# One core, attention and MLP: the first pair's decay inside its q k product, and a new order of the early loads

## The chip, the core and the metric

The kernel runs on one core of a Trainium2 chip. The core has a TensorE (PE, matrix products, with its weight loads PEld), a VectorE (DVE), a ScalarE (ACT), a GpSimd (POOL) and a SyncE (SP). POOL and SP issue the DMA transfers of this kernel; transfers from POOL may change the type from float32 to float16 on the way, those from SP may not. The metric is the device time in microseconds (us) of one execution, the median of several.

## The reference

For each of 8 batches and 8 heads (sequence S = 576, head size D = 64):

```python
scores = scale * np.matmul(q, k.transpose(0, 1, 3, 2))
log_f = np.log(np.clip(f, 0.0001, 1.0))
cum = np.cumsum(log_f, axis=-1)
decay = cum[:, :, :, None] - cum[:, :, None, :]
scores = np.where(causal, -1000000000.0, scores + decay)
attn = softmax(scores)            # exp(scores - max) / (sum + 1e-09)
x = (attn @ v), heads side by side: 4608 rows of 512
h = x @ w_in                      # 512 -> 2048
out = (h - np.tanh(h)) @ w_out    # 2048 -> 512
```

So a score of query s and key t needs q.k, plus a number that depends on s alone (cum at s), minus one that depends on t alone (cum at t).

## The kernel before, in words

**Pairs and tiles.** The work of attention is cut into 32 pairs: batch b, heads 2c and 2c+1. The scores of a pair lie with keys on partitions, in seven tiles `ti` of up to 512 columns (`TILES`, L289: tiles 0 to 2 are head 0, tile 3 holds the last 64 keys of both heads, tiles 4 to 6 are head 1). `scores` (L306) writes one tile into one of two PSUM buffers with PE and lets ACT take the exponential (L335). In batch 0 the causal mask is added by PE (a product of the identity with `late`, L329); later batches are masked by POOL. `trans` (L254) transposes q or k of the next pair on PE and has the result copied to `QT` and `KT` (L275 on ACT, L277 on DVE). `values` (L350) multiplies by v and `turn` (L369) transposes the result for the MLP.

**Decay.** f of all 64 batch-heads is loaded at once (L123), clipped (L150), put through Ln (L157) and summed along the sequence (a scan, L159). From `cum` come three rows for every head: `chi` (cum times 8, in float16), `clo` (what float16 lost of it) and `cq` (for the query side). For every pair but the first, these rows are copied by DMA into rows 64 to 66 of `KT` and `QT` (`load_aug`, L168), beside rows of 1 and -1 (`const_rows`, L175), and one product over 67 rows gives q.k and decay together. The first pair can't wait for that transfer: there `decay_part` (L294) adds the decay in two more products per piece of a tile (L295 with `dec`, which holds chi and clo for all heads, and a two-column selector `sel`; L297 with `cq` and a column of the identity), and the product of q and k (L326) has 64 rows.

**Order.** From `start` (L521) on, all five engines execute exactly in the order in which the program issues (`manual_schedule`, L604, L606); the lines above it (loads, constants, Ln, scan) are ordered by the scheduler. `unread(n)` (L512) issues n products of a constant tile that nobody reads, where PE would otherwise stand idle. `att_items` (L547) lists the work of pair p: while the scores of pair p are made, the transposes of pair p+1 (at tiles `at_q`, `at_k`) and the values of pair p-1 go in between, and `LOADS` (L196) says at which tile which load is issued by POOL. From pair 4 on, products of the MLP are dealt among the items (`TAKE`, L601).

**Loads.** POOL issues loads one after the other. There are eight completion semaphores for its transfers, used in turn, so that the ninth transfer waits until the first has landed. In the prologue POOL issues q and k of heads 0-1 and 2-3, the v parts of the first heads, then (`bulk`, L181) q of heads 4-7, the three rows of decay, k of heads 4-7 and four blocks of v. Then come, by `LOADS`, q and k of batch 1, the first half of `w_in` (`win`, 1024 KB), v of batch 1, the second half of `w_in`, `w_out`.

Of the kernel before, what the change touches and what calls it, by code (L numbers as in the profile page):

```python
# [14 lines left out]
PITCH = 640  # L15
# [6 lines left out]
def kernel(  # L22
# [95 lines left out]
    def load_v_block(b, n, h0, h1):  # L118
# [3 lines left out]
    lf = TQ[0][0:NH, :, :].rearrange("p c s -> p (c s)").bitcast(FP32)[:, 0:S]  # L122
    nc.sync.dma_start(out=lf, in_=f.rearrange("b h s -> (b h) s"))  # L123
    load_qk(qn, q, 0, 0, 2)
    load_qk(kn, k, 0, 0, 2)
# [4 lines left out]
    nc.gpsimd.affine_select(out=id16, in_=id16, compare_op=ALU.not_equal,  # L130
                            fill=1.0, base=0, pattern=[[-1, P]], channel_multiplier=1)
    load_qk(qn, q, 0, 2, 4)
    load_qk(kn, k, 0, 2, 4)
    ones16 = TK[0:NH, 0, :]
    sel = cst.tile([P, 2], FP16)
    dec = cst.tile([P, PITCH], FP16)
# [5 lines left out]
    nc.vector.memset(dec[:, S:PITCH], 0.0)  # L142
# [6 lines left out]

    nc.vector.tensor_scalar(out=lf, in0=lf, scalar1=0.0001, scalar2=1.0,  # L150
                            op0=ALU.max, op1=ALU.min)

    nc.vector.scalar_tensor_tensor(out=sel, in0=id16[:, 0:2], scalar=-1.0, in1=id16[:, NH:NH + 2],
                                   op0=ALU.mult, op1=ALU.subtract)
    nc.vector.memset(vn[0][D:P, NJ - 1, :, :], 0.0)
    nc.vector.memset(vn[0][:, :, :, D:VW], 1.0)
    nc.scalar.activation(out=lf, in_=lf, func=AF.Ln)  # L157
    cum = TQ[0][0:NH, :, :].rearrange("p c s -> p (c s)").bitcast(FP32)[:, S:2 * S]
    nc.vector.tensor_tensor_scan(out=cum, data0=ones16, data1=lf, initial=0.0,  # L159
                                 op0=ALU.mult, op1=ALU.add)  # L160
    chi = dec[0:NH, 0:S]
    nc.vector.tensor_scalar_mul(out=chi, in0=cum, scalar1=inv_qscale)
    cq = cst.tile([NH, S], FP16)
    expo = cst.tile([1, 1], FP32)
    clo = dec[NH:2 * NH, 0:S]
    nc.vector.scalar_tensor_tensor(out=clo, in0=cum, scalar=inv_qscale, in1=chi,
                                   op0=ALU.mult, op1=ALU.subtract)
    def load_aug(b):  # L168
        i, hs = b % 2, slice(b * H, (b + 1) * H)
        eng = nc.gpsimd if b == 0 else nc.sync  # L170
        eng.dma_start(out=KT[i][D:D + 1, :, 0:S], in_=chi[hs, :])
        eng.dma_start(out=QT[i][D + 2:D + 3, :, :], in_=cq[hs, :])
        eng.dma_start(out=KT[i][D + 1:D + 2, :, 0:S], in_=clo[hs, :])
# [7 lines left out]
    def bulk():  # L181
        load_qk(qn, q, 0, 4, H)
# [111 lines left out]
    def decay_part(ps, a, j, i0, n, col):  # L294
        nc.tensor.matmul(out=ps[:, col:col + n], lhsT=dec[:, j * P:(j + 1) * P],  # L295
                         rhs=sel[:, a:a + 1].to_broadcast([P, n]), start=True, stop=False)
        nc.tensor.matmul(out=ps[:, col:col + n], lhsT=id16[0:NH, a:a + 1].to_broadcast([NH, P]),  # L297
                         rhs=cq[:, i0:i0 + n], start=False, stop=False)

    FIRST = []  # L300

    def decay(ti):
        FIRST.append(ps_sc.tile([P, 512], FP32, tag="sc", name="ps"))
        decay_part(FIRST[0], *TILES[ti][0])

    def scores(b, c, ti):  # L306
        if FIRST:
            ps = FIRST.pop()
        elif b == 0 and ti == LAST:
# [9 lines left out]
        own = b == 0 and c == 0  # L319
        rows = D if own else D + 3  # L320
        for a, j, i0, n, col in TILES[ti]:
            h = 2 * c + a
            if own and ti > 0:
                decay_part(ps, a, j, i0, n, col)
            cut = min(P, n) if b == 0 and i0 == j * P else 0
            nc.tensor.matmul(out=ps[:, col:col + n], lhsT=KT[b % 2][0:rows, h, j * P:(j + 1) * P],  # L326
                             rhs=QT[b % 2][0:rows, h, i0:i0 + n], start=not own, stop=cut == 0)
            if cut:
                nc.tensor.matmul(out=ps[:, col:col + cut], lhsT=id16, rhs=late[:, 0:cut],  # L329
                                 start=False, stop=True)  # L330
# [4 lines left out]
        nc.scalar.activation(out=e[:, lo:hi], in_=ps[:, lo:hi], func=AF.Exp, scale=qscale)  # L335
# [185 lines left out]
    def start():  # L521
        unread(33)
        q_rest = trans(*pairs[0], qn, QT, True, "AAAA", True)
        nc.scalar.activation(out=cq, in_=cum, func=AF.Copy, bias=-SHIFT * inv_qscale, scale=inv_qscale)
        nc.scalar.activation(out=expo, in_=lf[0:1, 0:1], func=AF.Exp)
        unread(6)
        k_rest = trans(*pairs[0], kn, KT, True, "VVVV", True)
# [7 lines left out]
        scores(*pairs[0], 1)  # L535
        q_rest[1]()
        for e in EL[0:2]:
            nc.vector.memset(e, 0.0)
        nc.vector.memset(KT[0][:, :, S:PITCH], 0.0)
# [7 lines left out]
    def att_items(p):  # L547
# [8 lines left out]
        for ti in range(len(TILES)):  # L556
# [5 lines left out]
            if early and p > 0 and ti in (0, 6):  # L562
                put(unread, 2)
# [4 lines left out]
            at_q, at_k = (1, 3) if p == 0 else (0, 1) if early else (0, 2) if p == NPAIR else (0, 3)  # L568
# [34 lines left out]
    FIVE = {PE, mybir.EngineType.Pool, mybir.EngineType.SP, mybir.EngineType.DVE, mybir.EngineType.Activation}  # L603
    with tc.manual_schedule(engines=FIVE):  # L604
        start()
    with tc.manual_schedule(engines=FIVE):  # L606
        bulk()
        for p in range(len(pairs) + 1):
            b, c = divmod(p, NPAIR)
            items = att_items(p)  # L610
            take = TAKE[p] if p < len(TAKE) else 8 - (p - len(TAKE)) % 2
            if p == 2 * NPAIR + 1:
                widen(1)
            mine = mlp[at:at + take]
            at += take
            first = 14 if p == NPAIR else 0
            if p == len(pairs):
                for fn, *args in mine[0:2]:
                    fn(*args)
                mine = mine[2:]  # L620
            given, n = 0, 0
            whole = sum(counts for _, counts in items)
            for emit, counts in items:
                emit()
                n += counts
                while n > first and given < len(mine) and given * (whole - first) < (n - first) * len(mine):
                    fn, *args = mine[given]
                    fn(*args)
                    given += 1
        widen(2)  # L630
        for fn, *args in mlp[at:]:
            fn(*args)
# [28 lines left out]
```

## Time and profile before

| what | value |
|---|---|
| median of 3 runs | 347.94 us (347.92 to 347.96) |
| the profiled execution, its own time | 347.95 us |
| its span in the profile | 346.2 us |
| PE busy | 335.2 us (97%) |
| DVE busy | 261.7 us (76%) |
| ACT busy | 232.6 us (67%) |
| POOL busy | 161.3 us (47%) |
| DMA, all queues | 38.80 MB, mean 112 GB/s |
| granted TensorE clock | 1.0 in every slice |

Between the span and the execution's own time lie 1.75 us. PE is busy nearly throughout, but a busy PE is not a PE at its peak: its products overlap and their ends are modelled. The first 5 us of the span hold the loads and the way from f to `cum`; the first pair lies at about 8 to 16 us, pairs 1 to 3 at 16 to 30 us, and from 32 us on the MLP is dealt in.

### The profile page before, as it was taken

The page shows a single profiled execution, that of the slowest core. Times are in us where ns is not written, and L with a number is a line of the kernel's source. Part 1 is how long each engine was busy: PE and PEld are TensorE (multiplying, and loading weights), DVE is VectorE, ACT ScalarE, POOL GpSimd, SP SyncE. Part 2 cuts the span into 40 slices and gives each one's busy share as a digit, 9 for nine tenths or more (in the row PEclk, how much of TensorE's full clock was granted, in tenths as well). Part 3 has the DMA queues.
Part 4 walks back from the last instruction along what each step waited for, and adds up shares of the span by engine and source line. Part 5 has one row for each costly group of instructions (what it writes and reads, how often), then busy time and mean ns, then how long its engine had stood idle before and what let it go on. Part 6 is the DMA issues. An engine that isn't in the chain of part 4 may idle for free.

```text
span 346.2 us, 8606 instructions
## 1 busy us (share of the span) xinstructions
PE 335.2 (97%) x3253; PEld 230.6 (67%) x3253; DVE 261.7 (76%) x504; ACT 232.6 (67%) x437; POOL 161.3 (47%) x319
## 2 busy tenths in 40 slices
PE   8988998889999999999999999999999999999995
PEld 7476554555578656865688888755875587487485
DVE  6599787564988788678867886788677766876874
ACT  5687886777897787778767876788548842632640
POOL 8974652676558655765577465742322210000000
PEclk9999999999999999999999999999999999999999
DMA  8999999999999999799979997991131013003003
GB/s 108 147 182 201 193 201 154 107 114 177 132 130 105 177 137 122 94 176 137 117 78 200 130 128 78 186 143 27 49 97 31 17 50 110 0 14 109 0 11 113
DMA packets 144877, 38.80 MB, mean 112 GB/s; under 512 B 128148, under 2 KB 143236, under 8 KB 144836
## 3 DMA queue, kind: packets, MB, share of 16 engines
q0 software_dynamic: 92480, 18.39, 69.7%
q1 hardware_dynamic: 52356, 19.88, 30.5%
q8 instruction: 25, 0.41, 0.5%
q14 instruction: 16, 0.13, 0.1%
HBM read 36.85 MB, written 9.44 MB: 134 GB/s over the span
## 4 chain that ended last, share of the span: by engine, by line
PE 87%; DVE 6%; ACT 4%; issue 1%; DMA 1%; ACTq 0%
PE hps L408 32%; PE ops L466 28%; PE ps L326 12%; PE av L357 8%; PE ops L442 3%; DVE gq L417 2%; ACT e L335 2%; DVE QT L277 2%; PE t L264 1%; DVE KT L277 1%; PE ps L329 1%; DMA TQ<-in_f_dram 1%; PE ps L297 1%; ACT QT L275 1%; ACT th L413 1%
## 5 line engine op out<-in xcount | busy, mean ns | idle before, releaser
L408 PE MATMUL hps<-XR,win 128*128 128x512 f16 (+1 forms) x640 | 140.9, 357 | 0.9 <-ACT XR L378 0.7
L413 ACT ACTIVATE th<-hps 128x512 f32<-128x512 f32 x144 | 86.9, 603 | 55.4 <-PE hps L408 54.6
L335 ACT ACTIVATE e<-ps 128x512 f16<-128x512 f32 x192 | 110.5, 598 | 14.1 <-PE ps L326 6.0
L417 DVE TENSOR_TENSOR gq<-hps,th 128x512 f16<-128x512 f32 x144 | 98.4, 688 | 26.0 <-ACT th L413 24.6
L345 POOL TENSOR_SCALAR_AFFINE_SELECT e<-e 128x128 f16<-128x128 f16 x168 | 60.4, 361 | 78.0 <-ACT e L335 76.1
L408 PEld LDWEIGHTS <-win 128*128 128x128 f16 x640 | 57.7, 97 | 48.4 <-issue 0.5
L326 PE MATMUL ps<-QT,KT 67*128 67x64 f16 (+5 forms) x384 | 77.9, 276 | 3.1 <-ACT e L335 1.7
L466 PEld LDWEIGHTS <-gq 128*128 128x128 f16 x640 | 60.4, 97 | 11.1
L466 PE MATMUL ops<-wout,gq 128*128 128x256 f16 x512 | 63.2, 272 | 0.0
L326 PEld LDWEIGHTS <-KT 67*128 67x128 f16 (+1 forms) x384 | 36.7, 98 | 25.5 <-DVE KT L277 1.6
L357 PEld LDWEIGHTS <-e 128*128 128x128 f16 x896 | 32.2, 97 | 3.9
L357 PE MATMUL av<-vn,e 128*128 128x65 f16 x896 | 33.6, 193 | 0.0
L119 POOL DMA_DIRECT2D vn<-in_v_dram x32 | 28.0, 878 | 8.7 <-DMA win<-in_moe_w_in_dram 4.1
L466 PE MATMUL ops<-W,sq 128*128 128x256 f16 x256 | 31.2, 272 | 0.0
L366 DVE TENSOR_TENSOR xn<-av,rs 128x640 f16<-128x640 f32 x32 | 26.4, 825 | 1.1
L466 PEld LDWEIGHTS <-sq 128*128 128x128 f16 x256 | 24.2, 98 | 3.4
L96 POOL DMA_DIRECT2D kn<-in_k_dram x25 | 21.2, 848 | 1.5 <-issue 1.3
L345 POOL TENSOR_SCALAR_AFFINE_SELECT el<-el 128x128 f16<-128x128 f16 x28 | 9.4, 334 | 26.9 <-ACT el L335 26.2
L96 POOL DMA_DIRECT2D qn<-in_q_dram x25 | 21.2, 848 | 1.3 <-issue 0.8
L364 DVE TENSOR_SCALAR rs<-av 128x10 f32<-128x10 f32 x32 | 5.2, 162 | 19.0 <-PE av L357 17.9
L277 DVE COPY QT<-t 64x576 f16<-64x576 f16 x18 | 14.5, 803 | 6.2 <-PE t L264 6.1
L277 DVE COPY KT<-t 64x576 f16<-64x576 f16 (+1 forms) x22 | 16.3, 739 | 3.8 <-PE t L264 3.6
(82 smaller groups left out, 307.5 us busy)
## 6 DMA issues: line engine op xcount, KB each, us to landing
out_dram<-ost SPq DMA_DIRECT2D x34, 256.0 KB
vn<-in_v_dram POOLq DMA_DIRECT2D x24, 128.0 KB, 5.6
qn<-in_q_dram POOLq DMA_DIRECT2D x20, 128.0 KB, 4.3
kn<-in_k_dram POOLq DMA_DIRECT2D x20, 128.0 KB, 4.6
win<-in_moe_w_in_dram POOLq DMA_DIRECT2D x2, 1024.0 KB, 14.8
wout<-in_moe_w_out_dram POOLq DMA_DIRECT2D x2, 1024.0 KB, 14.1
XR<-xn SPq DMA_TRANSPOSE x56
vn<-in_v_dram POOLq DMA_DIRECT2D x12, 64.0 KB, 5.2
```

What stands on the lines that cost most here:

```text
L96: nc.gpsimd.dma_start(out=dst[b % 2][0:pn, n, :].rearrange("p (h d) -> p h d", h=H), in_=src[b, :, n * P:n * P + pn, :].rearrange("h p d - ...
L119: nc.gpsimd.dma_start(out=vn[b % 2][:, n, h0:h1, 0:D], in_=v[b, h0:h1, n * P:(n + 1) * P, :].rearrange("h p d -> p h d"))
L277: nc.vector.tensor_copy(out=to, in_=of)
L326: nc.tensor.matmul(out=ps[:, col:col + n], lhsT=KT[b % 2][0:rows, h, j * P:(j + 1) * P], rhs=QT[b % 2][0:rows, h, i0:i0 + n], start=not ow ...
L335: nc.scalar.activation(out=e[:, lo:hi], in_=ps[:, lo:hi], func=AF.Exp, scale=qscale)
L345: nc.gpsimd.affine_select(out=view, in_=view, compare_op=ALU.is_ge, fill=0.0, base=0, pattern=pat, channel_multiplier=-1)
L357: nc.tensor.matmul(out=av[:, a, ib, :], lhsT=E.pop((b, c, a, j, ib)), rhs=vn[b % 2][:, j, 2 * c + a, 0:D + 1], start=(j == 0), stop=(j == ib))
L366: nc.vector.tensor_tensor(out=xn.rearrange("p i (a d) -> p a i d", a=2), in0=av[:, :, :, 0:D], in1=rs.to_broadcast([P, 2, NJ, D]), op=ALU. ...
L408: nc.tensor.matmul(out=hps[:, o:o + n], lhsT=win[:, ci, ft * P:(ft + 1) * P], rhs=XR[:, ci, t:t + n], start=(ci == 0), stop=(ci == NCH - 1))
L413: nc.scalar.activation(out=th, in_=hps, func=AF.Tanh, scale=-1.0)
L417: nc.vector.tensor_tensor(out=GQ[(u, i)][:, half, kt, :], in0=hps, in1=th, op=ALU.add)
L466: nc.tensor.matmul(out=ps[:, m, :], lhsT=LHS[lhs](u, kt // 4)[:, kt % 4, m * P:(m + 1) * P], rhs=rhs[:, kt, :], start=(fresh and (apart or ...
```

## The change

**The first pair's decay.** `dec`, `sel`, `decay_part` and the twelve pairs of products L295 and L297 are gone. The first pair gets operands of its own: `KS` (in the space of W1) and `QS` (in the space of W2), 64 rows of transposed k or q and 24 rows of decay, 88 in all. The 24 rows are three for each of batch 0's eight heads: f is loaded a second time (from SP), each of the eight rows three times, into rows 64 to 87 of `lf`, and clip, Ln, scan and `chi` now work on 88 rows. A column of numbers per row (`per`, made by DVE from the identity) turns each of the 24 rows into what it must be: on the key side in one DVE operation for both heads (copied for head 1), on the query side in one ACT operation per head (`row_q`), where all rows but those of its own head come out as zero.

**Order of the prologue.** It is now all in program order: the identity is made before POOL's first load; Ln's table is loaded by a tiny activation at once, and Exp's table right behind Ln. `clo` for the other pairs is computed later, behind the first K copies, and in `bulk` its row and that of `cq` are issued behind the first two blocks of v. `unread` counts are new: 47, 6, 38, and four at each of four places in pair 0 (before: 33, 6, 22, 8).

**Loads of batch 1.** Of q and k of batch 1 heads 2-3 are loaded first, then the first half of `w_in`, and only then heads 4-7; v of batch 1 and the second half of `w_in` follow one step later each. In pair 1 the transposes of k come at tile 3 (before: 1).

```diff
+    NX = NH + 3 * H
+    lf = TQ[0][0:NX, :, :].rearrange("p c s -> p (c s)").bitcast(FP32)[:, 0:S]
+    nc.sync.dma_start(out=lf[0:NH, :], in_=f.rearrange("b h s -> (b h) s"))
+    nc.sync.dma_start(out=lf[NH:NX, :], in_=bass.AP(f.tensor, f.offset, [[S, H], [0, 3], [1, S]]))
+    expo = cst.tile([1, 1], FP32)
+    nc.scalar.activation(out=expo, in_=warm[0:1, 0:1], func=AF.Ln)
...
+    for to, g in ((isb, 1), (isc, 2)):
+        nc.vector.tensor_reduce(out=to, in_=id16[0:NX, NH + g:NX:3], op=ALU.add, axis=mybir.AxisListType.X)
...
+    nc.vector.memset(vn[0][:, :, :, D:VW], 1.0)
+    for h, (mul, add) in enumerate(((mul_0, add_0), (mul_1, add_1))):
+        nc.vector.tensor_scalar_mul(out=mul, in0=column(1, h), scalar1=inv_qscale)
+        nc.vector.scalar_tensor_tensor(out=add, in0=mul, scalar=-SHIFT, in1=column(0, h), op0=ALU.mult, op1=ALU.add)
+        nc.vector.tensor_tensor(out=add, in0=add, in1=column(2, h), op=ALU.subtract)
     nc.scalar.activation(out=lf, in_=lf, func=AF.Ln)
+    nc.scalar.activation(out=expo, in_=lf[0:1, 0:1], func=AF.Exp)
...
-    nc.vector.tensor_scalar_mul(out=chi, in0=cum, scalar1=inv_qscale)
-    nc.vector.scalar_tensor_tensor(out=clo, in0=cum, scalar=inv_qscale, in1=chi, ...
+    nc.vector.tensor_scalar(out=chi, in0=cum, scalar1=mul_k, scalar2=add_k, op0=ALU.mult, op1=ALU.add)
+    nc.vector.scalar_tensor_tensor(out=KS[NH:NX, 0, 0:S], in0=cum[NH:NX, :], scalar=mul_l[NH:NX, :], in1=chi[NH:NX, :],
...
     def bulk():
         load_qk(qn, q, 0, 4, H)
-        load_aug(0)
+        nc.gpsimd.dma_start(out=k_hi, in_=chi_0)
         load_qk(kn, k, 0, 4, H)
         for n in range(NJ - 1):
             load_v_block(0, n, 2, H)
+            if n == 1:
+                for to, of in rest:
+                    nc.gpsimd.dma_start(out=to, in_=of)
...
-             (0, 4): [lambda: load_qk(qn, q, 1, 2, H)],
-             (1, 0): [lambda: load_qk(kn, k, 1, 2, H)],
-             (1, 2): [lambda: load_win(0, DFF // 2)],
-             (1, 5): [lambda: load_v_rest(1), lambda: load_v_head(1, 0)],
-             (2, 1): [lambda: load_v_head(1, 1), lambda: load_win(DFF // 2, DFF)],
+             (0, 4): [lambda: load_qk(qn, q, 1, 2, 4), lambda: load_qk(kn, k, 1, 2, 4)],
+             (1, 0): [lambda: load_win(0, DFF // 2)],
+             (1, 2): [lambda: load_qk(qn, q, 1, 4, H)],
+             (1, 5): [lambda: load_qk(kn, k, 1, 4, H)],
+             (2, 1): [lambda: load_v_rest(1), lambda: load_v_head(1, 0)],
+             (2, 4): [lambda: load_v_head(1, 1), lambda: load_win(DFF // 2, DFF)],
...
-            if own and ti > 0:
-                decay_part(ps, a, j, i0, n, col)
-            nc.tensor.matmul(out=ps[:, col:col + n], lhsT=KT[b % 2][0:rows, h, j * P:(j + 1) * P],
+            nc.tensor.matmul(out=ps[:, col:col + n], lhsT=kt[0:rows, h, j * P:(j + 1) * P],
...
     def start():
+        def row_q(h, mul, add):
+            nc.scalar.activation(out=QS[NH:NX, h, :], in_=cum[NH:NX, :], func=AF.Identity, bias=add[NH:NX, :], scale=mul[NH:NX, :])
+
-        unread(33)
+        unread(47)
+        row_q(0, mul_0, add_0)
...
-        unread(22)
-        decay(0)
-        unread(8)
+        unread(38)
         scores(*pairs[0], 0)
+        row_q(1, mul_1, add_1)
+        unread(4)
+        nc.vector.scalar_tensor_tensor(out=clo, in0=cum[0:NH, :], scalar=inv_qscale, in1=chi[0:NH, :], op0=ALU.mult, op1=ALU.subtract)
+        nc.vector.tensor_copy(out=KS[NH:NX, 1, 0:S], in_=KS[NH:NX, 0, 0:S])
```

More of the change, by code (lines that the diff above doesn't have):

```diff
@@ L131 @@
                             fill=1.0, base=0, pattern=[[-1, P]], channel_multiplier=1)
+    load_qk(qn, q, 0, 0, 2)
+    load_qk(kn, k, 0, 0, 2)
     load_qk(qn, q, 0, 2, 4)
     load_qk(kn, k, 0, 2, 4)
-    ones16 = TK[0:NH, 0, :]
-    sel = cst.tile([P, 2], FP16)
-    dec = cst.tile([P, PITCH], FP16)
+    ones16 = TK[0:NX, 0, :]
     nc.vector.memset(ones16, 1.0)
@@ L141 @@
     nc.vector.memset(late, 0.0)
-    nc.vector.memset(dec[:, S:PITCH], 0.0)
+    nc.vector.memset(KT[0][:, :, S:PITCH], 0.0)
+    chi = cst.tile([NX, S], FP16)
+    clo = cst.tile([NH, S], FP16)
+    cq = cst.tile([NH, S], FP16)
+    KS = W1.rearrange("p k e -> p (k e)")[:, 0:2 * PITCH].rearrange("p (a n) -> p a n", a=2)
+    QS = W2.rearrange("p k e -> p (k e)")[:, 0:2 * S].rearrange("p (a n) -> p a n", a=2)
+    nc.vector.memset(KS[0:NX, :, S:PITCH], 0.0)
+    per = cst.tile([NX, 9], FP32)
+    nc.vector.memset(vn[0][D:P, NJ - 1, :, :], 0.0)
+    isb, isc, mul_k, add_k, mul_l, mul_0, add_0, mul_1, add_1 = (per[:, i:i + 1] for i in range(9))
     EL = [cst.tile([P, 192], FP16, tag=f"el{i}", name=f"el{i}") for i in range(3)]
@@ L163, with aug_rows @@
[L163 to L166, printed above, removed]
+    nc.vector.tensor_scalar(out=chi, in0=cum, scalar1=mul_k, scalar2=add_k, op0=ALU.mult, op1=ALU.add)
+    nc.vector.scalar_tensor_tensor(out=KS[NH:NX, 0, 0:S], in0=cum[NH:NX, :], scalar=mul_l[NH:NX, :], in1=chi[NH:NX, :],
                                    op0=ALU.mult, op1=ALU.subtract)
+    def aug_rows(b):
+        i, hs = b % 2, slice(b * H, (b + 1) * H)
+        return [(KT[i][D:D + 1, :, 0:S], chi[hs, :]), (KT[i][D + 1:D + 2, :, 0:S], clo[hs, :]), (QT[i][D + 2:D + 3, :, :], cq[hs, :])]
@@ L168, in load_aug @@
     def load_aug(b):
[L169 to L173, printed above, removed]
+        for to, of in aug_rows(b):
+            nc.sync.dma_start(out=to, in_=of)
     def const_rows(i):
@@ L292 @@
              4: (0, 1, 1, P), 5: (0, 1, 1, P), 6: (0, 2, 320, P)}
[L294 to L304, printed above, removed]
     def scores(b, c, ti):
-        if FIRST:
-            ps = FIRST.pop()
-        elif b == 0 and ti == LAST:
+        if b == 0 and ti == LAST:
             ps = ps_tr.tile([P, UW], FP32, tag="tr", name="ps")
@@ L318, in scores @@
         hi = max(x[4] + x[3] for x in TILES[ti])
-        own = b == 0 and c == 0
-        rows = D if own else D + 3
+        kt, qt, rows = (KS, QS, NX) if b == 0 and c == 0 else (KT[b % 2], QT[b % 2], D + 3)
         for a, j, i0, n, col in TILES[ti]:
             h = 2 * c + a
-            if own and ti > 0:
-                decay_part(ps, a, j, i0, n, col)
             cut = min(P, n) if b == 0 and i0 == j * P else 0
-            nc.tensor.matmul(out=ps[:, col:col + n], lhsT=KT[b % 2][0:rows, h, j * P:(j + 1) * P],
-                             rhs=QT[b % 2][0:rows, h, i0:i0 + n], start=not own, stop=cut == 0)
+            nc.tensor.matmul(out=ps[:, col:col + n], lhsT=kt[0:rows, h, j * P:(j + 1) * P],
+                             rhs=qt[0:rows, h, i0:i0 + n], start=True, stop=cut == 0)
             if cut:
@@ L535, in start @@
         scores(*pairs[0], 1)
+        unread(4)
         q_rest[1]()
@@ L561, in att_items @@
                 items.append((lambda: load_aug(1), False))
-            if early and p > 0 and ti in (0, 6):
-                put(unread, 2)
+            if early and ti in (0, 6) or p == 0 and ti == 5:
+                put(unread, 2 if p else 4)
             if p == 1 and ti == 3:
@@ L602 @@
     at = 0
[L603 to L632, printed above, removed]
+    start()
+    bulk()
+    for p in range(len(pairs) + 1):
+        b, c = divmod(p, NPAIR)
+        items = att_items(p)
+        take = TAKE[p] if p < len(TAKE) else 8 - (p - len(TAKE)) % 2
+        if p == 2 * NPAIR + 1:
+            widen(1)
+        mine = mlp[at:at + take]
+        at += take
+        first = 14 if p == NPAIR else 0
+        if p == len(pairs):
+            for fn, *args in mine[0:2]:
+                fn(*args)
+            mine = mine[2:]
+        given, n = 0, 0
+        whole = sum(counts for _, counts in items)
+        for emit, counts in items:
+            emit()
+            n += counts
+            while n > first and given < len(mine) and given * (whole - first) < (n - first) * len(mine):
+                fn, *args = mine[given]
+                fn(*args)
+                given += 1
+    widen(2)
+    for fn, *args in mlp[at:]:
+        fn(*args)
 _INS = ['q', 'k', 'v', 'f', 'moe_w_in', 'moe_w_out']
```

28 lines of the change are left out of this document (13 added, 15 removed).

## The prediction

> **What bounds the kernel now.** I read the chain that ended last first, to see whether the first 20 us lie on it at all; then the same chain in order of time, the timeline of PE and PEld in the first pair, the landing times of POOL's transfers, and what the DMA engines moved meanwhile.
>
> The page's chain, by engine and by line:
>
> ```profile
> PE 87%; DVE 6%; ACT 4%; issue 1%; DMA 1%; ACTq 0%
> PE hps L408 32%; PE ops L466 28%; PE ps L326 12%; PE av L357 8%; PE ops L442 3%; DVE gq L417 2%; ACT e L335 2%; DVE QT L277 2%; PE t L264 1%; DVE KT L277 1%; PE ps L329 1%; DMA TQ<-in_f_dram 1%; PE ps L297 1%; ACT QT L275 1%; ACT th L413 1%
> ```
>
> One transfer alone stands on it, that of f. All else is engines, in their written order. So a microsecond saved before pair 1 stays saved, unless a load becomes late. The chain in order of time, columns start and length:
>
> ```profile
> 0.81 2.71 DMA TQ<-in_f_dram
> ...
> 4.83 1.36 DVE TQ L159
> 6.21 0.72 DVE dec L162
> 6.96 0.75 DVE dec L166
> ...
> 16.39 0.22 PE ps L326
> 16.61 0.06 PE ps L329
> ...
> 18.70 0.45 PE av L357 x15
> 19.15 0.22 PE ps L326
> 19.36 0.07 PE ps L329
> 19.44 0.02 issue
> 19.46 0.61 ACT e L335
> ```
>
> The reader is to see three stretches: f to `dec` (to 7.7), the first pair, where PE is the chain from 7.96 to 16.39, and pair 1, which begins at 16.39 and in which PE stays the chain until the exponential of tile 4 at 19.46. Why PE is that slow in the first pair, the timeline shows (start, length, engine, line; in brackets the idle time before):
>
> ```profile
> 14.20 0.09 PEld L297 LDWEIGHTS <-id 64*128 64x128 f16 x1 [0.24 <-issue]
> ...
> 14.68 0.10 PEld L329 LDWEIGHTS <-id 128*128 128x128 f16 x1 [0.37 <-issue]
> ```
>
> A weight load of 64 rows behind products of 128 rows, or the reverse, is not made ahead: 0.24 to 0.42 us of PEld idle each. Behind products of 67 rows (from 16.2) no such gap stands. In the chain, the mask product L329 takes 0.16 in the first pair and 0.06 in pair 1.
>
> **What is removed.** Twelve pairs of products L295 and L297, and these switches: all products now have 88 to 128 rows. PE's part of the first pair shrinks from the 7.25 us between 9.14 and 16.39 to its columns: seven tiles with masks, two sets of transposes and 16 unread products, together 7,552 columns at 0.22 per 512, 3.2 us. So PE is no longer the bound there; three others are to be summed: the way of the new operands (DVE, ACT), and the transfers that pair 1 needs.
>
> **The start, worked out.** In front of clip there is a second load of f. SP's issue of the first takes 0.61 (0.81 to 1.42), so the second lands between 3.52 (beside the first) and 1.42 + 2.71 = 4.13; I take 4.13, as it is the same kind of transfer. Clip 0.54, to 4.68; Ln 0.68, to 5.39. Beside Ln, DVE has a memset (0.12) and six operations on one column, ahead of the scan: 0.09 (the memset of 128x32) to 0.16 (`sel`, 128x2) each and some 0.04 for each of four waits, so done between 5.50 and 5.92; I take 5.7, in the middle, since neither row is the same operation. That is 0.3 beyond Ln. Scan 1.35, to 7.05; chi 0.71; the low part 0.75; the first two K copies of 0.49: 9.55. `sel` (0.16) falls away. The first scores start at 9.6, against 9.14: **0.46 later**. Bounds: 8.7 (second f free, columns within Ln) and 9.9. The 38 unread products at 0.063 (1.39 for 22) behind the k transposes end before it. The identity made ahead of POOL's first load costs that load up to 0.4 (0.32 by its row and its wait), of which nothing is seen: q's copies now stand behind `row_q` on ACT, which needs the scan, and POOL's third load had the identity before it already. Ln's table was loaded at 0.81 before too, so the tiny activation gains nothing; Exp's table (1.28) now lies beside the scan and was beside the K copies: nothing.
>
> **The first pair on ACT and DVE.** ACT: first exponential at 9.6 + 0.38 + 0.06 + 0.05 = 10.1; then, in its order, exp 0.60, `row_q` 0.66 (row of `cq`, the nearest), QT copy 0.49, exp 0.60, QT copy 0.49, exp 0.60, 0.28, and three of 0.60: the last but one ends at 15.0, the last at 15.6. DVE from 9.55: `clo` 0.75, the copied rows some 0.4 (bounds 0.25 and 0.5, a memset and a copy of similar size), K copies 0.98, memsets 0.24, pair 1's QT 1.61 and KT 1.60: 15.15. So by the engines pair 1 can begin at **15.15**; before, 16.39.
> `row_q` has a scale and a bias per row, and `cq` has none. The Trainium skill (ScalarE: Activation LUTs, What ACT_TABLE_LOAD costs) says that each operand of one number per partition adds about 93 ns to an activation. By it the second `row_q` would take 0.85 and the last but one exponential end at 15.2 instead of 15.0. No trace here has such an activation; the sum does not need it.
>
> **The rows that pair 1 waits for.** Its products have 67 rows and need chi, clo and cq in `KT` and `QT`. Before, all three were issued ahead of k of heads 4-7; now clo and cq stand behind k and two blocks of v, each of which also waits for an older transfer's semaphore. Issue to landing, the last column:
>
> ```profile
> KT<-dec POOLq DMA_DIRECT2D x1, 9.0 KB, 4.7
> ```
>
> ```profile
> vn<-in_v_dram POOLq DMA_DIRECT2D x2, 96.0 KB, 5.2
> ```
>
> The first is clo, issued at 9.46 and landed at 14.2, long before it was needed. The second are the first two v blocks (issued 10.65 and 11.5): the second lands at 16.6. In the new order POOL reaches chi at 7.8, k at 8.4, the first v block at 9.46 (when q of heads 2-3 lands, as clo did), the second at 10.3, clo at 11.15 (computed at 10.3) and cq at 11.7. Bounds for cq: 11.7 + 3.8 (the first load, into empty queues) = 15.5, and 11.7 + 5.3 = 17.0 (a v block's landing). Between them: up to and with cq the same bytes are asked for as before up to the second v block, landed at 16.6. But before there was a hole, while POOL waited with clo (last column GB/s):
>
> ```profile
> 10.50:11.00 0.50, 0.50 (x11) 0.41 (x9) 0.00 (x0) 0.45 (x2) 0.50 (x2) 1.00 1.16 197
> 11.00:11.50 0.50, 0.50 (x5) 0.11 (x2) 0.39 (x1) 0.48 (x2) 0.50 (x2) 1.00 0.48 68
> 11.50:12.00 0.50, 0.50 (x5) 0.22 (x4) 0.49 (x2) 0.36 (x1) 0.50 (x2) 1.00 0.89 97
> 12.00:12.50 0.50, 0.50 (x8) 0.34 (x6) 0.50 (x1) 0.21 (x1) 0.50 (x2) 1.00 0.53 65
> 12.50:13.00 0.50, 0.50 (x11) 0.41 (x10) 0.21 (x1) 0.44 (x2) 0.50 (x1) 1.00 1.23 189
> ```
>
> From 11.0 to 12.5 it moved 115 KB where 290 went at 195 GB/s: 0.9 us lost. K of heads 4-7 issued over a microsecond earlier fills it, so cq lands at 16.6 - 0.9 = **15.7**. That is later than 15.15: PE waits 0.55 us for it, with the transposes of pair 2 queued behind, and ACT runs dry.
>
> **The sum.** PE starts at 15.75, and a product on an idle PE takes its 0.38, the mask 0.06: tile 0 of pair 1 is done at 16.19, before at 16.67. From there to the exponential of tile 4 PE executes the same work (the k transposes in another place), 2.8 us without a wait. So **0.48 us are saved**. Of the 1.24 that the engines offer, the transfer eats the rest.
>
> **Loads of batch 1: nothing.** In the first half of `w_in` (issued 16.67, landing 13.8 later, 30.5) there were 1.5 us to its first use at 31.98; 576 KB now come behind it. Q and k of heads 4-7 have the same bytes ahead as `w_in` had, so land at about 30.5, and are transposed in pair 5, at 40. POOL's mask of pair 4 waits, as before, behind a v block that waits for the transfer landing at 30.5; values read it a pair later. If that cover went, up to 0.5 us of mask time would show. The SP rows for batch 1 come later than 6.95 to 8.9, needed from 30.
>
> The profiled execution took 347.95 (span 346.25 and 1.7 around it), as good as the median 347.94. 347.95 - 0.48 = 347.47, say **347.45**.
>
> **Rivals.** By 0.2% I mean 0.70 us, about what a measurement can tell from no change.
> - *A, the sum above*, with cq landing between 15.3 and 16.3: 347.0 to 348.0. Chance 0.45, of which 0.17 beyond 0.7 faster.
> - *B, the rows land in time* (by 15.2, if the rows' few packets pass v's): pair 1 begins at 15.2, tile 0 done at 15.65, a gain of 1.0: 346.95. For it: chi, cq and clo landed 0.3 to 0.8 apart, so are cheap themselves. Against: eight transfers in flight took 4.7 to 5.6 each. Chance 0.20.
> - *C, the rows come late*: one mechanism, at the first tile of pair 1. cq issued at 11.8 and landing like a v block (5.3) comes at 17.1; tile 0 done at 17.6, 0.9 later than before: 348.9. It decides from a landing at 16.2, and beyond 0.2% from 16.9. For it: v blocks have the smallest packets, and the load of f adds bytes ahead. Against: the hole. Chance 0.17.
> - *D, the clock*: PE has 3.2 us of work in the six before pair 1, where it had none free before. In the first 4.9 us a product of 128 columns took 0.112, later 0.063; if it falls back to that, pair 1's 2.8 us of PE double at worst. I put 1.5 us on it: 349.5. No idle stretch in this trace is long enough to show such a fall. Chance 0.10.
>   The Trainium skill (TensorE: Matmul & The Clock Gate, Part 1) has the array at half its clock after an idle window of about 3.4 us; my longest idle stretch of PE is 2 us (10.9 to 13), so by that rule D does not come; the trace agrees on the warm-up, and can't show the fall.
> - *E, the start is as late as 1 us* (f's second load and the columns both at their upper ends or beyond), so that the engines begin pair 1 at 15.8 to 16.4 and the gain is gone: 347.9. Chance 0.08. That the removed products were not on the path is excluded by the chain.
>
> **Chances.** Faster by over 0.2%: B and 0.17 of A, 0.37. Within: the rest of A and E, 0.36. Slower: C and D, 0.27. The range 346.8 to 348.9 leaves out D, a third of C and a little of B; A's own range is 347.0 to 348.0.
>
> **What would show it.** Right: first scores at 9.4 to 9.8; no L329 weight load with an idle of 0.2 or more in the first pair; PE's first product of 67 rows waiting for a transfer into QT or KT, at 15.4 to 16.2; cq issued at 11.5 to 12. Wrong: that product waiting for DVE or ACT instead (E or B), or a product of 128 columns at 0.11 us after 10 us (D), or a wait for `win` or for q, k of batch 1 at 30 to 42 us.

## The result: 1.4 us slower

Over 19 runs of each, the changed kernel takes 349.37 us (348.86 to 353.05), the kernel before 347.95: a ratio of 1.0053, with a 95% interval of 1.0037 to 1.0069. Here and below the time is the median, the ratio is near that of the means (here 349.79 and 347.95), so a few long runs move the ratio and not the time. Forecast were 347.45 and a range of 346.8 to 348.9. The profiled execution took 349.56 us, 1.61 more than the one of before.

The page's chain of after, by engine and by line:

```profile
PE 84%; DVE 6%; ACT 3%; DMA 3%; issue 1%; POOL 1%; SPq 0%; ACTq 0%; DVEq 0%
PE hps L416 32%; PE ops L474 28%; PE ps L334 11%; PE av L365 8%; PE ops L450 3%; DVE gq L425 2%; ACT e L343 2%; DVE QT L302 2%; DMA QT<-cq 1%; DMA TQ<-in_f_dram 1%; PE t L289 1%; DVE KT L302 1%; ACT QT L300 1%; ACT th L421 1%; DVE xn L374 0%
```

Two things are new in it: `QT<-cq`, the row for which pair 1 waits, and POOL. DMA has gone from 1% to 3%, PE from 87% to 84%. The chain of after in order of time (start, length) shows how the two are tied:

```profile
0.81 0.61 SPq L126
...
1.48 4.30 DMA TQ<-in_f_dram
...
5.88 0.46 DVE TQ L171
...
7.43 1.28 DVE TQ L181
8.71 0.03 issue
8.73 0.59 DVE chi L183
9.32 0.28 issue
9.60 0.53 POOL KT L204
10.13 0.69 POOL kn L90
...
12.47 0.52 POOL KT L210
12.99 4.65 DMA QT<-cq
17.64 0.24 issue
17.88 0.38 PE ps L334
```

f's second load lands at 5.78 (forecast 4.13), so clip, scan and `chi` are late; `chi` holds POOL, on which its row, k and two blocks of v are queued ahead of clo and cq; and cq's row, issued at 12.99, lands at 17.64. PE appears in this chain only at 17.88. Its waits in the meantime, in the timeline (idle time before and its releaser in brackets):

```profile
11.21 0.39 PE L334 MATMUL ps<-W,W 88*128 88x512 f16 x1 [1.47 <-DVE W L302]
...
14.68 0.19 PE L334 MATMUL ps<-W,W 88*128 88x64 f16 x1 [1.19 <-ACT W L300]
...
17.88 0.38 PE L334 MATMUL ps<-QT,KT 67*128 67x512 f16 x1 [1.04 <-DMA QT<-cq]
```

Later in the same chain:

```profile
18.31 0.11 PE idle L523 x2
...
21.10 0.61 ACT e L343
```

Tile 0 of pair 1 is done at 18.31, before at 16.67: 1.64 later, which is the whole difference of the two executions (1.61). The exponential of tile 4 follows 2.79 later in both (21.10 behind 18.31, 19.46 behind 16.67). So everything that was lost was lost before tile 0 of pair 1 was done.

### The profile page after: what moved, and what is told of

It reads as the page before. It is cut to its first block, busy times and chain, and to the rows that moved or that the text cites. A ratio compares the mean times of both kernels' runs of the same rounds, so it can differ in the third digit from the quotient of the medians.

```text
span 347.8 us, 8662 instructions
## 1 busy us (share of the span) xinstructions
PE 333.2 (96%) x3271; PEld 232.2 (67%) x3271; DVE 263.8 (76%) x516; ACT 234.5 (67%) x440; POOL 162.3 (47%) x321
## 4 chain that ended last, share of the span: by engine, by line
PE 84%; DVE 6%; ACT 3%; DMA 3%; issue 1%; POOL 1%; SPq 0%; ACTq 0%; DVEq 0%
PE hps L416 32%; PE ops L474 28%; PE ps L334 11%; PE av L365 8%; PE ops L450 3%; DVE gq L425 2%; ACT e L343 2%; DVE QT L302 2%; DMA QT<-cq 1%; DMA TQ<-in_f_dram 1%; PE t L289 1%; DVE KT L302 1%; ACT QT L300 1%; ACT th L421 1%; DVE xn L374 0%
## 5 line engine op out<-in xcount | busy, mean ns | idle before, releaser
L425 DVE TENSOR_TENSOR gq<-hps,th 128x512 f16<-128x512 f32 x144 | 98.5, 688 | 26.1 <-ACT th L421 24.6
L334 PE MATMUL ps<-QT,KT 67*128 67x512 f16 (+1 forms) x372 | 74.6, 276 | 4.1 <-ACT e L343 1.7
L334 PEld LDWEIGHTS <-KT 67*128 67x128 f16 x372 | 35.5, 98 | 26.6 <-DVE KT L302 2.8
L489 ACT ACTIVATE m<-ops 128x512 f32<-128x512 f32 x16 | 9.5, 596 | 10.9 <-PE ops L474 10.9
```

The costliest lines, as they stand in the source:

```text
L334: nc.tensor.matmul(out=ps[:, col:col + n], lhsT=kt[0:rows, h, j * P:(j + 1) * P], rhs=qt[0:rows, h, i0:i0 + n], start=True, stop=cut == 0)
L425: nc.vector.tensor_tensor(out=GQ[(u, i)][:, half, kt, :], in0=hps, in1=th, op=ALU.add)
```

## The experiments

Theory: two things are late, the start (f's second load) and the rows of clo and cq behind two blocks of v, and PE standing for them can let its clock fall. Rivals: only one of the two counts; the loads of batch 1 or the new place of k's transposes cost the time; the new operations themselves cost it.

**The second load away.**

```diff
-    nc.sync.dma_start(out=lf[NH:NX, :], in_=bass.AP(f.tensor, f.offset, [[S, H], [0, 3], [1, S]]))
...
     nc.vector.tensor_scalar_mul(out=mul_l, in0=isc, scalar1=inv_qscale)
+    nc.vector.memset(lf[NH:NX, :], 0.9)
```

> The changed kernel without the second load of f: its 24 rows are a constant 0.9 written by DVE ahead of clip (so the first pair's decay is wrong, all work is kept). Theory 1 (the second load, landed at 5.8 where 4.1 was forecast, is the whole loss): clip starts at about 4.1, the first scores at 9.4 to 9.6 instead of 11.2, cq is issued at about 11.7 and lands at 15.5 to 16.3, time 347.2 to 347.9, no slower than before. Theory 2 (the rows clo and cq behind two blocks of v are a loss of their own): cq lands at 16.9 or later, pair 1 begins there, time 348.4 to 348.9.

Measured: 351.41 us, ratio 1.01 (1.0083 to 1.0118). Neither time was expected: it is slower than the change itself. The start was earlier (first scores at 9.93, against 11.21), but cq, issued at 11.70, landed 5.6 later, at 17.3, as theory 2 had it (16.9 or later), so that PE stood from 15.55 to 17.53. Then the granted clock fell, which neither theory had. Stretches of this run (start and end, length, PE busy with the number of its products, granted clock, DMA share, GB/s):

```profile
12.50:15.90 3.40, 2.01 (x25) 1.00 1.91 152
15.90:19.30 3.40, 1.73 (x28) 1.00 1.40 156
19.30:22.70 3.40, 3.25 (x42) 0.50 1.06 172
22.70:26.10 3.40, 3.40 (x31) 0.50 1.10 183
26.10:29.50 3.40, 2.94 (x55) 1.00 1.38 180
```

The reader is to see the granted clock, behind the number in brackets: half from 19.3 to 26.1, behind 3.4 us in which PE was busy 1.73.

**The order of the two loads swapped.** Is it the shape of the second load (24 rows that read each row of f three times) or its place?

```diff
-    nc.sync.dma_start(out=lf[0:NH, :], in_=f.rearrange("b h s -> (b h) s"))
     nc.sync.dma_start(out=lf[NH:NX, :], in_=bass.AP(f.tensor, f.offset, [[S, H], [0, 3], [1, S]]))
+    nc.sync.dma_start(out=lf[0:NH, :], in_=f.rearrange("b h s -> (b h) s"))
```

> The changed kernel with the two loads of f in the other order: the repeated 24 rows first, the 64 rows second. Theory C (what is issued second meets POOL's loads of q and k on the same engines): the 64 rows land late now, clip starts at 5 or later, time 349.0 to 349.7 as the changed kernel. Theory S (the form of the repeated load, eight rows outermost, is slow by itself): the 24 rows land at 3.3 to 4.3 from the head of the queue or the 64 rows land by 4.3, clip starts at 4.0 to 4.4, time 347.4 to 348.2.

Measured: 349.37 us, 1.0055 (1.0028 to 1.0083), as the change. Now the plain load of 64 rows is the second, and it is the late one:

```profile
1.75 3.85 DMA TQ<-in_f_dram
```

In the kernel before the same load, issued first, took 2.71. So the shape is not needed for a late load: the place is enough. Both kernels' q and k loads on POOL start at 1.4 to 1.6; that the second load meets their packets is a likely cause, but only argued, as the first load was also still under way then. How late it comes differs: with the same order of loads, the 24 rows took 4.30 in the change and 3.70 in a run further below.

**The second load on ACT's queue.**

```diff
-    nc.sync.dma_start(out=lf[NH:NX, :], in_=bass.AP(f.tensor, f.offset, [[S, H], [0, 3], [1, S]]))
+    nc.scalar.dma_start(out=lf[NH:NX, :], in_=bass.AP(f.tensor, f.offset, [[S, H], [0, 3], [1, S]]))
```

> The changed kernel with the repeated load of f issued by ACT, beside SP's first load, instead of behind it. Theory C: both loads are ahead of POOL's, land by 3.5 to 4.0, the first scores start at 9.4 to 9.7, time 347.2 to 348.0; Ln's table load moves behind the issue (0.6) and still ends before clip. Theory S: the repeated rows land at 5 or later all the same, time 348.8 to 349.5.

Measured: 350.24 us, 1.0074 (1.0056 to 1.0093). The start is mended (clip at 3.72, first scores at 9.06, against 9.14 before), and yet the kernel is slower, for the same two reasons as without the load: cq, issued at 11.19, took 5.4 to land, so pair 1 began late, and the clock fell. The timeline, and the stretches:

```profile
16.82 0.38 PE L334 MATMUL ps<-QT,KT 67*128 67x512 f16 x1 [2.14 <-DMA qn<-in_q_dram]
```

```profile
11.00:14.40 3.40, 2.06 (x29) 1.00 1.79 172
14.40:17.80 3.40, 1.26 (x19) 1.00 1.70 152
17.80:21.20 3.40, 3.36 (x48) 0.50 1.07 159
21.20:24.60 3.40, 3.00 (x41) 1.00 1.09 200
```

The wait is put down to a load of q; but q of batch 1 is not an operand of this product. Cq landed at 16.6, and the product follows it by the same 0.24 as in the change. Whether it was the second queue or the issue 0.67 us earlier (0.81, against 1.48) that mended the start, this run does not separate.

**The loads of batch 1 and k's transposes alone**, in the kernel before:

```diff
-             (0, 4): [lambda: load_qk(qn, q, 1, 2, H)],
-             (1, 0): [lambda: load_qk(kn, k, 1, 2, H)],
-             (1, 2): [lambda: load_win(0, DFF // 2)],
+             (0, 4): [lambda: load_qk(qn, q, 1, 2, 4), lambda: load_qk(kn, k, 1, 2, 4)],
+             (1, 0): [lambda: load_win(0, DFF // 2)],
+             (1, 2): [lambda: load_qk(qn, q, 1, 4, H)],
...
-            at_q, at_k = (1, 3) if p == 0 else (0, 1) if early
+            at_q, at_k = (1, 3) if p == 0 else (0, 3) if p == 1 else (0, 1) if early
```

> The kernel before with nothing but the new order of batch 1's loads (heads 4-7 of q and k behind the first half of w_in) and the k transposes of pair 1 at tile 3. Forecast: nothing, 347.9 to 348.0, no PE wait for a load between 16 and 60 us. Rival (a load of batch 1 or v becomes late, or the transposes in their new place cost the 0.26 us that they filled): 348.1 to 348.6.

Measured: 348.19 us, 1.0006 (0.9995 to 1.0018). By the interval that is not to be told from nothing, but one or two long runs on each side make the interval wide: nine of its ten runs took 348.15 to 348.19, where twelve of the fourteen of the kernel before took 347.93 to 348.01. So it is 0.2 slower, as the rival with the transposes had it. In its profile the exponential of tile 4 begins at 19.67 instead of 19.46, as k's transposes stand between the values there; no wait for a load appears.

**Both late things mended**: the load on ACT's queue, and the rows ahead of all blocks of v.

```diff
-    nc.sync.dma_start(out=lf[NH:NX, :], in_=bass.AP(f.tensor, f.offset, [[S, H], [0, 3], [1, S]]))
+    nc.scalar.dma_start(out=lf[NH:NX, :], in_=bass.AP(f.tensor, f.offset, [[S, H], [0, 3], [1, S]]))
...
         load_qk(kn, k, 0, 4, H)
+        for to, of in rest:
+            nc.gpsimd.dma_start(out=to, in_=of)
         for n in range(NJ - 1):
             load_v_block(0, n, 2, H)
-            if n == 1:
-                for to, of in rest:
-                    nc.gpsimd.dma_start(out=to, in_=of)
```

> The changed kernel with the second load of f issued by ACT, and with the rows of clo and cq issued by POOL right behind k of heads 4 to 7, ahead of all blocks of v. Theory (late start plus rows behind two blocks of v): in the run with ACT's queue clo was computed at about 9.8, so its row is issued at about 9.9 and that of cq at 10.4; at the 4.6 to 5.3 us that such a row took there, cq lands at 15.0 to 15.7, pair 1 begins at 15.0 to 15.7 and its tile 0 is done by 15.5 to 16.2 instead of 16.67 before: 346.8 to 347.5 us, plus 0.2 for the transposes of k in their new place, 347.0 to 347.7, if the granted clock holds. Rival 1: rows land late wherever they stand (16.5 or later), tile 0 done at 17.0, 348.5. Rival 2: PE is so sparse in the first pair that the clock falls all the same, 349 to 350.5, with 0.5 in the rows of the granted clock behind 16 us.

Measured: 346.77 us, 0.9967 (0.9955 to 0.9979): faster than the kernel before, and 0.2 below the theory's range (347.0 to 347.7). The landing of cq (KB, us to landing) and the chain of its profile:

```profile
QT<-cq POOLq DMA_DIRECT2D x1, 9.0 KB, 3.7
```

```profile
14.87 0.03 issue
14.89 0.39 PE ps L333
15.28 0.06 PE ps L336
15.34 0.11 PE idle L522 x2
```

Cq is issued at 10.81 and landed at 14.5 (the theory had 15.0 to 15.7), before it is needed; tile 0 of pair 1 is done at 15.34, 1.33 earlier than before.

**The rows mended alone**: the second part of that diff, without the first.

> The changed kernel with one thing moved: the rows of clo and cq are issued by POOL right behind k of heads 4 to 7, ahead of all blocks of v; f is loaded as in the change. Theory: chi's row is issued at 9.6 as in the change, k at 10.1, clo at about 11.0 to 11.5 (it is computed by about 11), cq at 11.5 to 12.0, landing at 16.1 to 16.6; pair 1 then waits for the copies of its own k (17.07 in the change) and not for rows, begins at 17.1 instead of 17.88, and the time is 349.4 - 0.8 = 348.6, so still slower than before by what the late start costs. Rival (the rows' place is nothing, the late start is all): as the change, 349.4. Rival (the blocks of v behind them become late): 349.4 or more, with a wait of av for vn in pair 0.

Measured: 347.65 us, 1.0004 (0.9989 to 1.0019): as the kernel before, 1.7 us faster than the change, and 0.95 faster than the theory gave. The expected limit at 17.1, the copies of pair 1's k, was taken from the change, where the first scores start at 11.21. In the profiled execution f's second load landed at 5.18 instead of 5.78, the first scores started at 10.76, and pair 1 at 16.42, without a wait for a row:

```profile
1.48 3.70 DMA TQ<-in_f_dram
...
10.76 0.39 PE ps L333
...
16.42 0.39 PE ps L333
```

That execution took 348.11, which is 1.45 less than the profiled one of the change. Of this, 0.45 lies ahead of the first scores, where the place of the rows can do nothing, and 1.0 behind them. Why the median is 0.46 lower still, this profile can't show.

**The clock by itself**: the kernel without the second load, with PE kept at work.

```diff
-                put(unread, 2 if p else 4)
+                put(unread, 2 if p else 40 if ti == 6 else 4)
```

> The kernel without the second load of f (its 24 rows of f are a constant 0.9, so the first pair's decay is not the reference's), with 36 unread products more behind tile 6 of pair 0, so that PE works through the stretch of 15.6 to 17.5 in which it stood waiting for the rows. The rows and all else keep their times. Theory (the clock falls because PE stands): the granted clock stays at 1.0 in all rows, tile 0 of pair 1 is done at about 18.0 instead of 16.67, and the time is 347.95 + 1.3 = 349.3, 2 us below the 351.4 that the same kernel took with PE standing. Rival (the clock falls for another reason, or the 2 us are a stall elsewhere): 351 or more.

Measured: 349.26 us, 1.0036 (1.0023 to 1.0049), as expected, 2.15 us less than without the filling, though pair 1 begins at the same time (17.57, against 17.53). First two stretches without the filling, then the same and the one between them with it:

```profile
15.50:17.50 2.00, 0.05 (x1) 1.00 1.80 143
19.30:22.00 2.70, 2.70 (x40) 0.50 1.06 171
```

```profile
15.50:17.50 2.00, 2.00 (x39) 1.00 1.75 147
17.50:19.30 1.80, 1.76 (x31) 1.00 1.18 162
19.30:22.00 2.70, 2.30 (x46) 1.00 1.12 184
```

Products whose results nobody reads save 2 us: what they save is the clock.

**The rows' place alone**, in the kernel before:

```diff
         load_qk(qn, q, 0, 4, H)
-        load_aug(0)
+        nc.gpsimd.dma_start(out=KT[0][D:D + 1, :, 0:S], in_=chi[0:H, :])
         load_qk(kn, k, 0, 4, H)
         for n in range(NJ - 1):
             load_v_block(0, n, 2, H)
+            if n == 1:
+                nc.gpsimd.dma_start(out=KT[0][D + 1:D + 2, :, 0:S], in_=clo[0:H, :])
+                nc.gpsimd.dma_start(out=QT[0][D + 2:D + 3, :, :], in_=cq[0:H, :])
```

> The kernel before with one thing of the change: the rows of clo and cq are issued behind k of heads 4 to 7 and two blocks of v instead of right behind that of chi. Theory (rows behind two blocks land 4.6 to 5.5 us after their issue): they are issued two to three us later than before and land at 16.0 to 17.0, so pair 1 begins at 16.4 to 17.0: 347.95 to 348.6. Rival (the rows' place costs what the change lost): 349.0 to 349.5. Rival (hidden): 347.95, as PE needs until 16.39 for the first pair anyway.

Measured: 348.02 us, 1.0008 (0.9991 to 1.0024): hidden by the median. In the profiled execution (347.92) cq is issued at 11.42 and lands 4.4 later, at 15.8; PE is busy with the first pair until 16.4. The late row costs only where PE would be ready for it. That little cover is left may be why four of the ten runs took 348.21 to 350.10, but they have no profile.

**The rows late, the start mended, the clock held**: the load on ACT's queue and the 36 products more.

> The changed kernel with the second load of f issued by ACT (rows of clo and cq still behind two blocks of v) and 36 unread products more behind tile 6 of pair 0, which fill the 2 us in which PE stood for the rows. Theory (rows late cost 0.6 us, the rest of the 350.24 us is the clock): the rows land at about 16.5 to 16.8 as without the filling, tile 0 of pair 1 is done at 17.2, the granted clock is 1.0 in all rows, and the time is 347.95 + 0.55 + 0.2 = 348.7. Rival (the clock is not the cause, or falls in spite of the filling): 350 or more.

Measured: 348.67 us, 1.0021 (1.0012 to 1.0030). Pair 1's first product starts at 16.82, to the hundredth as without the filling, and the clock stays:

```profile
14.40:17.80 3.40, 3.33 (x55) 1.00 1.88 143
17.80:21.20 3.40, 2.96 (x59) 1.00 1.07 154
```

So of the 2.3 us by which the kernel with ACT's queue was behind, 0.7 are the rows (and k's place), and 1.6 the clock.

**Two more steps from the better version.** First, k's transposes in pair 1 back at tile 1:

```diff
-            at_q, at_k = (1, 3) if p == 0 else (0, 3) if p == 1 else (0, 1) if early
+            at_q, at_k = (1, 3) if p == 0 else (0, 1) if early
```

> The version with f's second load issued by ACT and the rows of clo and cq ahead of v, and in pair 1 the transposes of k back at tile 1, where the kernel before has them. Theory (the 0.2 us by which the loads and k's place alone were slower came from that place): 346.77 - 0.2 = 346.55 us, pair 1's exponential of tile 4 about 0.2 us earlier behind its tile 0 than in the version with the transposes at tile 3. Rival (the place is nothing): 346.77. Rival (k of heads 4 and 5 or its copies are late at tile 1, as PE comes there 1.5 us earlier than before): a wait in front of these transposes or of pair 2's first scores, 347.0 or more.

Measured: 346.72 us, 0.9962 (0.9949 to 0.9974). In the profile the exponential of tile 4 comes 2.59 behind tile 0 (17.67 behind 15.08) instead of 2.79, as the theory has it, but the median moved by 0.05 only (the profiled execution is the fastest of the five, 346.35); 346.77 and 346.72 are not to be told apart. This is the best version run, 1.25 us below the kernel before. No transfer stands on its chain any more:

```profile
PE 86%; DVE 7%; ACT 5%; issue 1%; ACTq 0%
```

Second, on top of it, ACT's list shortened: `row_q` of head 1 ahead of the first exponential, cq by DVE.

```diff
-        nc.scalar.activation(out=cq, in_=cum[0:NH, :], func=AF.Copy, bias=-SHIFT * inv_qscale, scale=inv_qscale)
+        row_q(1, mul_1, add_1)
...
         nc.vector.scalar_tensor_tensor(out=clo, in0=cum[0:NH, :], scalar=inv_qscale, in1=chi[0:NH, :], op0=ALU.mult, op1=ALU.subtract)
+        nc.vector.tensor_scalar(out=cq, in0=cum[0:NH, :], scalar1=inv_qscale, scalar2=-SHIFT * inv_qscale, op0=ALU.mult, op1=ALU.add)
```

> The version with f's second load issued by ACT, the rows ahead of v and k's transposes at tile 1, with ACT's list between the first exponential and the fourth tile shortened: the query rows of head 1 are made ahead of that exponential, and cq by DVE behind clo. ACT had 0.86 us for these rows between the exponentials of tile 0 and 1, and the first pair waits for ACT there (1.19 us of PE idle at 11.5 to 12.7). Theory: tile 3's wait ends 0.7 us earlier; the row of cq is then issued at 11 to 11.4 and lands at 14.7 to 15.3, so pair 1 begins 0 to 0.4 us earlier and the time is 346.2 to 346.55. Rival (rows are the bound again, or DVE, which has the 0.6 us more, becomes it): 346.6 to 347.

Measured: 347.20 us (346.58 to 351.48), 1.0002 (0.9975 to 1.0029). The wait for ACT shrank as expected, from 1.19 to 0.18, but the time went into a wait for DVE, and the spread grew: the four runs of 348.15 and more have a mean granted clock of 0.985 to 0.995. Where in them it fell is not shown, as the profiled execution has 1.0 throughout; its two waits:

```profile
11.84 0.19 PE L333 MATMUL ps<-W,W 88*128 88x64 f16 x1 [0.18 <-ACT W L299]
...
15.01 0.39 PE L333 MATMUL ps<-QT,KT 67*128 67x512 f16 x1 [1.01 <-DVE KT L301]
```

**The four cells.** Start and rows, each late or mended; the runs at the four medians have a mean granted clock of 0.999 or 1.0:

| | rows behind two blocks of v | rows ahead of v |
|---|---|---|
| second load on SP's queue | 349.37 (the change) | 347.65 |
| second load on ACT's queue | 348.67 (PE filled) | 346.77 |

By these medians the rows' place is worth 1.72 and 1.90 us, the load's queue 0.70 and 0.88, so the two add up within the scatter of the runs. With the load on SP's queue the traces show only 1.0 for the rows, as said above: there the landing of f's second load differs from one execution to the next. The new operations themselves do not cost the time: the version at 346.77 has all of them.

## Why the prediction was wrong

The step that failed is "**cq lands at 15.7**" (bounds 15.5 and 17.0). It landed at 17.64, beyond both bounds, and tile 0 of pair 1 was done at 18.31 instead of the 16.19 of the sum: 2.12 too late, of which 1.94 is the landing, and 0.19 that the product follows a landing by 0.24 and not by 0.05. The 1.94 has two parts.

- *1.29 of the issue* (12.99, forecast 11.7). It comes from "**I take 4.13, as it is the same kind of transfer**" for f's second load: it landed at 5.78, 1.65 later. The swapped order shows that its shape is not the reason, and the load on ACT's queue that it can land in time. The upper bound was the first load's own duration behind SP's issue, as if a load issued 0.67 later, behind another, took as long as the first; the nearest row of the kernel before, POOL's first load of q (144 KB, issued at 1.41, 3.8 to landing), would have given 1.42 + 3.8 = 5.2. What slows a load in that place stays open. 0.36 of the 1.65 were given back between that landing and cq's issue, as POOL needed 3.4 from the row of `chi` to that of cq (9.60 to 12.99) and not 3.9.
- *0.65 of the flight* (4.65, forecast 4.0). The reckoning by the hole in the DMA traffic (0.9 us of bytes filled, so cq 0.9 earlier than v before) has no support: behind two blocks of v cq took 4.4 to 5.7 in seven kernels, between and beyond the 3.8 and 5.3 that were named as its bounds; ahead of v it took 3.0 and 3.7, but in the kernel before, ahead of k and v and 2.3 to 4.1 us earlier, 5.1. So what sets the flight of such a row is not settled by its place alone. The nearest row was not used: cq's own in the kernel before (first line; the second is the change), by which it would have landed at 11.7 + 5.1 = 16.8.

```profile
QT<-cq POOLq DMA_DIRECT2D x1, 9.0 KB, 5.1
```

```profile
QT<-cq POOLq DMA_DIRECT2D x1, 9.0 KB, 4.6
```

**Rival C** is what came: "the rows come late", cq forecast at 17.1 and the time at 348.9; measured 17.64 and 349.37. Its condition (beyond 0.2% from a landing at 16.9) was right. It was given 0.17, with the load of f named in its favour, and that load was then left at its early value: two unknowns were bounded one by one, but both ends hung together, since a late f moves cq's issue as well. The range stopped at 348.9, short of the two upper ends taken at once.

Point by point, the rest:

- *The start*, +0.46 by the sum (first scores at 9.6; bound 9.9): 11.21 measured, +2.07. With the load on ACT's queue it is 8.98 to 9.40 in five versions, below the sum and within its bounds. The six column operations lay beyond Ln as forecast; the difference is the load. **Rival E** (a start up to 1 us late) understated it.
- *The first pair on ACT and DVE*: right as a length, with the wrong engine as its only bound. From first scores to pair 1's first product the sum had 5.55 (9.6 to 15.15), on DVE; it is 5.65 or 5.66 in the three versions with early rows (9.24 to 14.89, 10.76 to 16.42, 8.98 to 14.63). There DVE's copies end just before that product, but the chain goes over ACT and `row_q` of head 1. `row_q` takes 0.86, not the 0.66 of the row taken: 0.18 more than `cq`'s 0.68 for two operands of one number per partition. That is what the Trainium skill (ScalarE: Activation LUTs, What ACT_TABLE_LOAD costs) states, about 93 ns for each; the trace agrees, and its 0.85 was the better number. Taken out from between the exponentials it gained next to nothing (5.61, 9.40 to 15.01), as cq, moved to DVE with it, lengthened the other path. In the version with both things mended it stands on the chain (start, length):

```profile
10.35 0.86 ACT W L530
```

- *The switches of row count*: right. The mask product L337 takes 0.06 in the first pair, where it took 0.16. (In the trace of before, weight loads show gaps of 0.16 to 0.42 at about half of the switches, not at each.) The engines' gain of 1.24 is real, and the mended versions have it: 1.18 us at 346.77. In the change it was paid away in the late start and the rows.
- *Loads of batch 1*: nothing, right; in no trace does PE wait for one of them between 8 and 60 us (where a wait is put down to one, it is for cq, as said above). The new place of k's transposes, also put at nothing, costs 0.2: alone it gave 348.19, and it is the 2.79 against 2.59 between tile 0 and tile 4.
- *Rival D, the clock*: in the profiled execution of the change it does not come, but in two of the experiments it does. Its size was near (1.5 us forecast, 1.6 and 2.15 measured between kernels with and without filling), in part by luck: the forecast had at most pair 1's 2.8 us of products slowed, the traces have 3.4 and 6.8 us. Its exclusion was wrong: "my longest idle stretch of PE is 2 us, so by that rule D does not come". Idle stretches of 1.98 and 2.14 were followed by half clock. The Trainium skill (TensorE: Matmul & The Clock Gate, Part 1) puts a window of about 3.4 us behind it. The length agrees, as the low stretches are 3.4 and 6.8 us long; but the windows before them were not idle: PE was busy 1.73 and 1.26 of 3.4 us in them. In the profiled execution of the change, where the clock held, PE was busy at least 1.87 of any 3.4 us from 8 to 21. Four of the 19 runs of the change, those of 350.49 to 353.05, have a mean clock of 0.985 to 0.995, so D had a part in the change's mean, though not in its median; where in them the clock fell is not shown.

## What to carry to other kernels

When work is taken off the bounding engine, list what the next engine-ready time is waiting for, and give each transfer the issue time and the flight time it has in the new order, both ends together; here a row of 9 KB that had landed 3 us before it was needed (issued at 8.24, 5.1 to landing, needed at 16.39) was issued 4.75 us later and became the bound. In this case it paid to issue the small load that stands in front of everything at once, on a queue of its own, and small rows ahead of the bulk loads on the queue that carries both. And a TensorE freed to stand about can lose its clock: compare with a version in which it is kept busy by unread products before the cost is put on the wait.

## What the runs showed of the hardware

- The same load of f (64 rows, 144 KB) took 2.71 us when issued first on SP and 3.85 when issued second, 0.9 us later; that of 24 rows, issued second, took 4.30 and 3.70 in two traces with the same order.
- TensorE's granted clock fell to 0.5 for 3.4 or 6.8 us behind stretches of 3.4 us in which PE was 37% and 51% busy, and not behind ones of 59% and 61%, in the two kernels shown, nor behind 55% (1.87 of 3.4 us) in the change; a stretch of that length without any work was not needed.
- The row of the granted clock does not show everything: in the kernel before it reads 1.00 in the first 5 us too, though 33 products of 128 columns took 3.70 us there, 0.112 each, and 22 of them 1.39, 0.063 each, from 6.5 on.
- The same row of 9 KB on POOL's queue took 3.0 to 5.7 us from issue to landing; its place among the bulk loads alone does not settle which.
